# Beginning of a fused attention and two-layer kernel: three weight units and the last tokens' scores are moved

## The chip, the cores and the metric

One core of one Trainium2 chip runs the whole program. The metric is the device time of one execution in microseconds: 1802.85 us for the kernel before, the median of 3 runs (1801.82 to 1803.31).

## What is computed

Attention with keys and values summed over 8 neighbouring positions, for 8 batches of 576 tokens and 8 heads of 64; its output, 4608 rows of 512, goes through a layer with g = h cos(h), and that through a gated layer. All arrays are float32.

```
k_p = mean of k over groups of 8 positions; v_p likewise        # (B, H, 72, 64)
scores = q @ k_p.T / sqrt(64);  attn = softmax(scores);  x = attn @ v_p
x -> (4608, 512)
h = x @ w_in        (512 x 2048);   y = (h * cos(h)) @ w_out    (2048 x 512)
z = (silu(y @ w_gate) * (y @ w_val)) @ w_out2
```

Here w_in and w_out matter. They arrive as 64-bit floats and are converted on the chip.

## The kernel before, in words

The tokens are worked on in blocks of 512 columns; the first block needs the attention of batch 0 (576 tokens). The program opens with that attention, then runs 9 x 16 "slots": slot (n, f) computes one block of h (128 rows of d_ff by 512 tokens) for token block n, its cosine, and two slots later the product with w_out.

**Conversion of weights.** A generator `conv` goes through a fixed list `order` of units of 128 x 512 values: units 0 to 7 are w_in (groups 0 and 1, four row blocks each), then units of w_out ("o") and of the rest of w_in ("i") alternate. A unit is loaded as pairs of 32-bit words by SP's queue (L459) into the place that its result will have, or into one of two raw buffers for w_out. VectorE then takes six steps for a unit of w_in: mask the exponent (L466), sign (L477), mask the mantissa (L483), low word (L488), product (L494), and the low part after ScalarE has cast the high part to fp32r (L998, L1011); between the first and the second, ScalarE does a bias step (L472). Units of w_out have the first five. `fill(m)` takes m steps of the generator, and `fill_to` runs it until a given unit is done. The first masking of a unit is begun up to two units ahead. In the first 16 slots each slot calls for 8 such steps and for one unit of w_out. Units below 8 use a buffer with the tag "w" (four of them), which the rounding of turns in each slot uses too.

**Opening.** Keys, values and q of batch 0 and 1 are loaded by SP; `load_kv1` loads k and v of batch 1 into places that later hold w_in's groups 2 and 3, so those units can be loaded only when these sums are done. Then the string `program` is worked through: "s" scores and exponentials of a tile of tokens (tile 4 is the last 64), "x" its normalisation, "p" transposes of weights, "a" attention output into `ring` (L382, copied at L388), "K" and "U" sums of batch 1's k and v, "f" and "F" conversion, "X" the cut of x into a high and a low part `xhl` (ScalarE L128, VectorE L129; four row blocks), "k" the transposes of batch 1's pooled k (`prep_k`, L231 to L238), "i", "o", "q" and "b" loads. Batch 1's attention runs inside slots 1 to 16.

**Slots.** `pe_h` (L532 to L534) makes h of three fp32r products into one of two banks "hg"; `turns` scales it (ScalarE L541, a single buffer "hs"), rounds (ScalarE L543, VectorE L544); `cosine` takes sine and square (ScalarE L565, L566) and the product with h (VectorE L569). `pe_y` (L595 in the first block) multiplies with w_out. Scores, transposed weights, attention outputs and `prep_k` share two banks "att".

**Order.** Each engine works off one queue in order. What stands in it is put in order beforehand by a planner, which goes through the instructions by written order and takes, for each engine, the first one that it believes ready; so an instruction can be placed ahead of one that was written earlier. `keep_in_program_order` keeps an instruction behind the one written before it on its engine.

Of the kernel before, what the change touches and what calls it, by code (L numbers as in the profile page):

```python
# [25 lines left out]
def fused_kernel(  # L26
# [18 lines left out]
    nc = tc.nc  # L45
# [4 lines left out]
    P = 128  # L50
    POOL = 8
    SP = S // POOL
    NP = H // 2
# [4 lines left out]
    KC = DM // P  # L58
# [19 lines left out]
    ident = const.tile([P, P], F32, name="ident")  # L78
# [48 lines left out]
    def split(hi, lo, src):  # L127
        nc.scalar.copy(hi, src)  # L128
        nc.vector.tensor_sub(lo, src, hi)  # L129
# [90 lines left out]
    def sum_kv(b, kind, i):  # L220
# [2 lines left out]
        dst = vps[b][:, i] if kind == "v" else kps[b][:, i] if i < NP else kps[b][: SL * NP, i]  # L223
        pool_sum(nc.gpsimd, dst, kvraw.pop((b, kind, i)))

    def prep_k(b):

        kp = kps.pop(b)
        ps = psum.tile([P, NP * SP], F32, name=f"kps_{b}", tag="att", bufs=2)
        for g in range(2):  # L230
            nc.tensor.transpose(ps[:, g * P : (g + 1) * P], kp[:, 2 * g : 2 * g + 2].rearrange("s r d -> s (r d)"), ident)  # L231
        m = SL * NP
        nc.tensor.transpose(ps[:, 2 * P :], kp[:m, NP:].rearrange("s r d -> s (r d)"), ident[:m, :m])
        for r in range(2):
            rows = slice(r * D, (r + 1) * D)
            to = kT[rows, :, r * SP : (r + 1) * SP]
            nc.scalar.mul(to[:, :, :SM], ps[rows, : 2 * P].rearrange("d (p s) -> d p s", p=NP), -EXP_SCALE)
            nc.scalar.mul(to[:, :, SM:], ps[rows, 2 * P :].rearrange("d (s p) -> d p s", p=NP), -EXP_SCALE)  # L238
# [104 lines left out]
    def do_pt(b, t):  # L343
        pth, ptl, ptx = av_tile("pth", b), av_tile("ptl", b), av_tile("ptx", b)
        t0, n = TILES[t]
        o = t0 - GROUPS[GROUP[t]][0]
        pm = pms.pop((b, t))
        ps = psum.tile([P, NP, n], F32, name=f"pt_{b}_{t}", tag="att", bufs=2)
        for p in range(NP):
            nc.tensor.transpose(ps[:, p], pm[:n, p * P : (p + 1) * P], ident[:n, :n])  # L350
        if b < ACTB:
            nc.scalar.copy(pth[:, :, o : o + n], ps)
            px = psum.tile([SM, n], F32, name=f"px_{b}_{t}", tag="att", bufs=2)
            nc.tensor.transpose(px, pm[:n, NP * P : NP * P + SM], ident[:n, :n])
            nc.scalar.copy(ptx[:SM, o : o + n], px)
            return
        nc.scalar.copy(pth[:, :, o : o + n], ps)
        nc.vector.tensor_sub(ptl[:, :, o : o + n], ps, pth[:, :, o : o + n])
        px = psum.tile([P, n], F32, name=f"px_{b}_{t}", tag="att", bufs=2)
        nc.tensor.transpose(px, pm[:n, NP * P :], ident[:n, :n])  # L360
        nc.scalar.copy(ptx[:, o : o + n], px)
        nc.vector.tensor_sub(ptx[SM:, o : o + n], px[SM:], ptx[SM:, o : o + n])
# [143 lines left out]

    xhl = []

    def x_split(half):
        if not xhl:  # L510
            xhl.append(const.tile([P, 2, KC, TB], F32R, name="xhl", tag="xhl"))
        for c in range(KC):
            src = ring[:, c, half * TB : (half + 1) * TB]
            split(xhl[0][:, 0, c], xhl[0][:, 1, c], src)

    wa = {}
    acc = {}
# [421 lines left out]
    order = [("i", j, c) for j in range(2) for c in range(KC)][: KC + LEAD]  # L939
# [6 lines left out]
    def load_i(m):  # L946
        for _ in range(m):
            u = next(to_load_i, None)
            if u is not None:
                _, j, c = order[u]  # L950
                cv_load(keys[u], w_in[c * P : (c + 1) * P, j * TB : (j + 1) * TB], f"wa{j}{c}")
# [24 lines left out]
    def conv():  # L976

        n = len(order)
        begun = 0
        x = None  # L980
        done = -1
        for u in range(n + 1):
            if u < n:
                while begun <= u:
                    first(begun)
                    begun += 1
                    yield done
                cv_sign(keys[u])
                yield done
            if u > 0:  # L990
                x = cv_mul(keys[u - 1])
                if order[u - 1][0] == "o":
                    load_o(1)
                    done = u - 1
                else:
                    _, j, c = order[u - 1]
                    home = wa[j, c] = wts.tile([P, 2, TB], F32R, name=f"wa_{j}_{c}", tag=f"wa{j}{c}")
                    nc.scalar.copy(home[:, 0], x)  # L998
                yield done
            if u < n:  # L1000
                cv_high(keys[u])
                yield done
            while begun < min(u + 3, n) and not (order[begun][0] == order[begun - 1][0] == "o"):
                first(begun)
                begun += 1
                yield done
            if u < n:
                cv_low(keys[u])
                yield done
            if u > 0 and order[u - 1][0] == "i":  # L1010
                nc.vector.tensor_sub(home[:, 1], x, home[:, 0])  # L1011
                done = u - 1
                yield done

    wo_raw = []
    conv_ops = conv()
    conv_done = [-1]

    def fill(m):
        for _ in range(m):  # L1020
            conv_done[0] = next(conv_ops, len(order))

    def fill_to(kind, j, c):
        u = order.index((kind, j, c))
        while conv_done[0] < u:
            fill(1)
# [21 lines left out]
        pool_sum(nc.vector, kps[0][:, 2 * g : 2 * g + 2], kst[:, 2 * g : 2 * g + 2])  # L1048
    pool_sum(nc.vector, kps[0][: SL * NP, NP:], kst[: SL * NP, NP:NK])
    prep_k(0)  # L1050
    load_kv1()
    load_i(1)
    fill(8)
    do_qt(0, 0)
    kfree = kst.rearrange("s h x -> s (h x)")
# [22 lines left out]
    def sum_v1():  # L1078
# [3 lines left out]


    program = (
        "s0 s1 f4 x0 s2 p0 V0 v x1 p1 f6 s3 F3 a0 x2 p2 x3 p3 a1 w K0 K1 K2 U0 X s4 q i11 o2 "
        "x4 k b f6 "
    )
    steps = {
        "s": s_,
# [6 lines left out]
        "U": lambda t: sum_v1(),  # L1096
        "f": fill,
        "F": lambda c: fill_to("i", 0, c),
        "i": load_i,
        "o": load_o,  # L1100
        "q": lambda: load_q(1),
        "k": lambda: prep_k(1),
        "b": lambda: load_kv(*raws[0]),
        "w": lambda: wo_raw.extend(
            p1w.tile([P, 8, DM], F32, name=f"wo_{i}", tag=f"big{i}", bufs=1) for i in range(2)
        ),
        "X": lambda: x_split(0),
    }
    for step in program.split():
        steps[step[0]](*([int(step[1:])] if step[1:] else []))  # L1110
# [15 lines left out]
    for i, s in enumerate(slots):  # L1126
        n, f = s
        if s == (NB - 1, 0):
            p1a.release()
            pools2["a"] = tc.alloc_tile_pool(name="p2a", bufs=1, reuse_waits="tile")  # L1130
            tsteps = t_steps(0)
            gsteps = None
        units1, units2 = units2, []
        if n == 0:
            if f % KC == 0:
                fill_to("i", f // KC, KC - 1)
            load_i(1)
        if i + 2 in cv_slots and i % NF1 != 1:
            w2_get()
        if f == 0 and i:  # L1140
            pe_y(slots[i - 2])
        pe_h(s)
        if 2 * NF1 <= i + 1 < len(slots):
            wo_load(i + 1)
        if n == 0:
            fill(4)
        turns(s)
        if 0 < i <= NF1:
            fill_to("o", 0, i - 1)
        if i:  # L1150
            parts(slots[i - 1])
        if f == NF1 - 1 and n + 1 < NB:
            x_split((n + 1) % 2)
        if n == 0:
            fill(2)
        for u in units1:
            cv_bias(u)
        if f == 1 and n:
            pe_y(slots[i - 2])
        run_slot(mids, i)  # L1160
        if f > 1 or i == 1:
            if i >= 2:
                pe_y(slots[i - 2])
        if n == 0:
            fill(2)
        cosine(s)
        if f == 1 and n:
            y_out(n - 1)
        for u in units1:
            nc.sync.dma_start(w2_dram[w2c], cv_val(u))  # L1170
            w2c += 1
        run_slot(lates, i)
        run_slot(exps, i)
        run_slot(norms, i)
        if n == 0:
            if i == 0:
                do_pt(0, 4)
                do_qt(1, 0)
                for p in range(NP):
                    do_av(0, 2, p)  # L1180
            if i == 2:
                prep_v(1)
        else:
            if i + 2 in cv_slots and i % NF1 == 1:
                w2_get()
            if i + 1 in cv_slots:
                units2 = [f"w2_{w2c}"]
        for u in units2:
            cv_exp(u)
        if i == 2 * NF1:  # L1190
            osteps = gen_out()
        if 64 <= i < 79 or 104 <= i < 119 or 127 <= i < 142:
            run(osteps)
        if n == NB - 1:
            if f == 1:
                load_x2(0)
            if f == 2:
                gen_load(0)
            if 3 <= f < 11:
                run(tsteps)  # L1200
            if f == 8:
                gsteps = gen_steps(0)
            if f >= 8:
                run(gsteps, 2)
# [80 lines left out]
```

## Time and profile before

| | |
|---|---|
| median of 3 runs | 1802.85 us |
| the profiled execution | 1801.87 us |
| its span in the trace | 1800.1 us |
| VectorE busy | 1247.9 us (69%) |
| ScalarE busy | 1075.4 us (60%) |
| granted TensorE clock, mean | 0.993 |

The trace holds one execution. "Busy" counts instructions at work, without waits. PE is TensorE, DVE VectorE, ACT ScalarE, POOL GpSimd, SP the engine that issues transfers. Times in rows count from the start of the span.

### The profile page before, as it was taken

The page shows a single profiled execution, that of the slowest core. Times are in us where ns is not written, and L with a number is a line of the kernel's source. Part 1 is how long each engine was busy: PE and PEld are TensorE (multiplying, and loading weights), DVE is VectorE, ACT ScalarE, POOL GpSimd, SP SyncE. Part 2 cuts the span into 40 slices and gives each one's busy share as a digit, 9 for nine tenths or more (in the row PEclk, how much of TensorE's full clock was granted, in tenths as well). Part 3 has the DMA queues.
Part 4 walks back from the last instruction along what each step waited for, and adds up shares of the span by engine and source line. Part 5 has one row for each costly group of instructions (what it writes and reads, how often), then busy time and mean ns, then how long its engine had stood idle before and what let it go on. Part 6 is the DMA issues. An engine that isn't in the chain of part 4 may idle for free.

```text
span 1800.1 us, 23553 instructions
## 1 busy us (share of the span) xinstructions
PE 1743.4 (97%) x8056; PEld 1443.0 (80%) x8056; DVE 1247.9 (69%) x2147; ACT 1075.4 (60%) x1956; POOL 139.1 (8%) x218
## 2 busy tenths in 40 slices
PE   5789999999999999999999999999999999999998
PEld 3446588788878888888878888888888888999998
DVE  6598787877777777787875586863684367458346
ACT  4588578777877767778676664533443344344333
POOL 0130410403103012000000000000000000000000
PEclk9889999999999999999999999999999999999999
DMA  9634244646566454584785488576567656787773
GB/s 219 175 106 120 79 169 138 202 132 205 141 195 229 114 200 128 165 239 142 235 274 177 165 319 288 196 258 222 190 201 265 197 190 221 294 261 246 294 253 91
DMA packets 245031, 357.03 MB, mean 198 GB/s; under 512 B 146480, under 2 KB 152624, under 8 KB 244912
## 3 DMA queue, kind: packets, MB, share of 16 engines
q1 hardware_dynamic: 240224, 354.35, 61.9%
q10 hardware_dynamic: 4688, 1.18, 0.3%
q8 instruction: 64, 1.05, 0.2%
q14 instruction: 55, 0.45, 0.1%
HBM read 285.74 MB, written 69.73 MB: 197 GB/s over the span
## 4 chain that ended last, share of the span: by engine, by line
PE 75%; DVE 11%; DMA 7%; ACT 5%; issue 1%; SPq 0%; DVEq 0%; ACTq 0%
PE X L787 14%; PE oX L917 8%; PE Y L787 7%; PE h L532 5%; PE h L533 5%; PE h L534 5%; PE acc L602 5%; PE acc L603 5%; PE acc L604 5%; PE oY L917 4%; PE Z L787 4%; PE av L382 3%; PE oZ L917 2%; PE s L297 2%; PE acc L595 2%; DMA w2r<-w_dram 2%
## 5 line engine op out<-in xcount | busy, mean ns | idle before, releaser
L532 PE MATMUL h<-xhl,wa 128*128 128x512 f32 x576 | 232.2, 403 | 10.0 <-ACT hs L541 10.0
L787 PE MATMUL X<-t_P,wc 128*128 128x512 f32 (+1 forms) x1080 | 232.7, 368 | 0.8 <-ACT u L836 0.8
L533 PE MATMUL h<-xhl,wa 128*128 128x512 f32 x576 | 226.1, 392 | 0.0
L534 PE MATMUL h<-xhl,wa 128*128 128x512 f32 x576 | 225.8, 392 | 0.0
L787 PEld LDWEIGHTS X<-t_P,wc 128*128 128x128 f32 x1080 | 196.5, 188 | 27.3 <-ACT u L836 2.1
L603 PE MATMUL acc<-gl,wo_ring 128*128 128x512 f32 x448 | 176.2, 393 | 3.3 <-DVE gl L583 3.2
L604 PE MATMUL acc<-gh,wo_ring 128*128 128x512 f32 x448 | 174.9, 390 | 0.0
L602 PE MATMUL acc<-gh,wo_ring 128*128 128x512 f32 x448 | 173.4, 400 | 0.9 <-ACT gh L580 0.6
L532 PEld LDWEIGHTS h<-xhl,wa 128*128 128x128 f32 x576 | 108.8, 189 | 36.8 <-ACT hs L541 11.6
L569 DVE SCALAR_TENSOR_TENSOR w<-w,hs 128x512 f32<-128x512 f32 x144 | 101.6, 706 | 49.2 <-ACT w L566 48.1
L541 ACT ACTIVATE hs<-h 128x512 f32<-128x512 f32 x144 | 85.8, 596 | 76.5 <-DVE w L569 51.7
L534 PEld LDWEIGHTS h<-xhl,wa 128*128 128x128 f32 x576 | 108.7, 189 | 23.6 <-issue 0.5
L565 ACT ACTIVATE w<-w 128x512 f32<-128x512 f32 x144 | 91.0, 632 | 61.0 <-DVE w L544 59.9
L533 PEld LDWEIGHTS h<-xhl,wa 128*128 128x128 f32 x576 | 109.0, 189 | 23.0 <-issue 1.9
L839 DVE TENSOR_TENSOR p<-p,X 128x512 f32<-128x512 f32 (+1 forms) x60 | 37.8, 632 | 117.1 <-PE X L787 109.6
L544 DVE SCALAR_TENSOR_TENSOR w<-w,hs 128x512 f32<-128x512 f32 x144 | 103.5, 719 | 21.9 <-ACT w L543 21.9
L583 DVE TENSOR_TENSOR gl<-w,gh 128x512 fp32r<-128x512 f32 x128 | 89.5, 699 | 41.9 <-ACT gh L580 40.6
L128 ACT CAST xhl<-pst 128x1024 fp32r<-128x1024 f32 (+1 forms) x70 | 67.7, 968 | 71.1 <-PE oX L917 26.1
L543 ACT ACTIVATE w<-hs,few 128x512 f32<-128x512 f32 x144 | 104.5, 725 | 9.6 <-DMA w_dram<-ce_w 4.7
L603 PEld LDWEIGHTS acc<-gl,wo_ring 128*128 128x128 f32 x448 | 84.2, 188 | 24.0 <-DVE gl L583 7.9
L917 PE MATMUL oX<-xhl,wc 128*128 128x512 f32 (+1 forms) x480 | 102.8, 368 | 0.0
L602 PEld LDWEIGHTS acc<-gh,wo_ring 128*128 128x128 f32 x448 | 83.7, 188 | 19.9 <-ACT gh L580 3.0
(202 smaller groups left out, 3558.2 us busy)
## 6 DMA issues: line engine op xcount, KB each, us to landing
wc<-wc_dram SPq DMA_DIRECT2D x273, 512.0 KB
wo_ring<-wo_dram SPq DMA_DIRECT2D x112, 512.0 KB
wc_dram<-wc SPq DMA_DIRECT2D x42, 512.0 KB
wc_dram<-ow SPq DMA_DIRECT2D x42, 256.0 KB
y_dram<-yo SPq DMA_DIRECT2D x18, 512.0 KB
w_dram<-ce_w SPq DMA_DIRECT2D x36, 256.0 KB
st_i<-in_moe_w_in_dram SPq DMA_DIRECT2D x16, 512.0 KB
st_o<-in_moe_w_out_dram SPq DMA_DIRECT2D x16, 512.0 KB
```

Source lines behind the costliest of these rows:

```text
L532: nc.tensor.matmul(ps, whi, xhl[0][:, 0, c], start=c == 0, stop=False)
L533: nc.tensor.matmul(ps, whi, xhl[0][:, 1, c], start=False, stop=False)
L534: nc.tensor.matmul(ps, wlo, xhl[0][:, 0, c], start=False, stop=c == KC - 1)
L543: nc.scalar.activation(w, h, AF.Identity, bias=magic)
L544: nc.vector.scalar_tensor_tensor(out=w, in0=w, scalar=MAGIC, in1=h, op0=ALU.subtract, op1=ALU.subtract)
L565: nc.scalar.activation(w, w, AF.Sin, scale=PI)
L569: nc.vector.scalar_tensor_tensor(out=w, in0=w, scalar=1.0, in1=h, op0=ALU.subtract, op1=ALU.mult, reverse0=True)
L602: nc.tensor.matmul(acc[n][i], a[:, cols], xh, start=f == 0, stop=False)
L603: nc.tensor.matmul(acc[n][i], a[:, cols], xl, start=False, stop=False)
L604: nc.tensor.matmul(acc[n][i], b[:, cols], xh, start=False, stop=f == NF1 - 1)
L787: nc.tensor.matmul(ps[:, :hb], w, t[:, x, c, :hb], start=first and c == 0 and n == 0, stop=c == 1 and n == 2, skip_group_check=not first,)
L917: nc.tensor.matmul(banks[key][m][:, :hb], u, x[:, b, i, :hb], start=first_ and j == i == k == 0, stop=j == NJ - 1 and i == 1 and k == 2, s ...
```

## The change

Units 4 to 6 of w_in are loaded ahead of `load_kv1` (one of them stood behind it, two were loaded by the conversion itself), unit 7 ahead of batch 1's q; "G2" converts up to unit 6 ahead of the sums K and U and the cut X. Until X is written, no unit beyond 7 is begun (`ahead`). The last 64 tokens' scores "s4" move from behind X to ahead of the attention output "a0". `prep_k(1)` moves from behind their normalisation to behind the first slot's products. Pinned to written order: the cuts of X on both engines, the transposes in `prep_k(1)`, and those of the last 64 tokens' weights.

```diff
+    def pinned(ins, cond):
+
+        if cond:
+            tc.keep_in_program_order(ins)
...
-            nc.tensor.transpose(ps[:, g * P : (g + 1) * P], kp[...], ident)
+            pinned(nc.tensor.transpose(ps[:, g * P : (g + 1) * P], kp[...], ident), b == 1)
...
-            nc.tensor.transpose(ps[:, p], pm[:n, p * P : (p + 1) * P], ident[:n, :n])
+            pinned(nc.tensor.transpose(ps[:, p], pm[:n, p * P : (p + 1) * P], ident[:n, :n]), (b, t) == (0, 4))
...
-    def x_split(half):
+    def x_split(half, first=False):
...
-            split(xhl[0][:, 0, c], xhl[0][:, 1, c], src)
+            a = nc.scalar.copy(xhl[0][:, 0, c], src)
+            b = nc.vector.tensor_sub(xhl[0][:, 1, c], src, xhl[0][:, 0, c])
+            if first:
+                tc.keep_in_program_order(a)
+                tc.keep_in_program_order(b)
...
-            while begun < min(u + 3, n) and not (order[begun][0] == order[begun - 1][0] == "o"):
+            while begun < min(u + 3, n, ahead[0]) and not (order[begun][0] == order[begun - 1][0] == "o"):
...
+    ahead = [2 * KC]
...
+    load_i(3)
     load_kv1()
-    load_i(1)
...
-        "s0 s1 f4 x0 s2 p0 V0 v x1 p1 f6 s3 F3 a0 x2 p2 x3 p3 a1 w K0 K1 K2 U0 X s4 q i11 o2 "
-        "x4 k b f6 "
+        "s0 s1 f4 x0 s2 p0 V0 v x1 p1 f6 s3 s4 F3 a0 x2 p2 x3 p3 a1 w i1 q G2 K0 K1 K2 U0 X i11 o2 "
+        "x4 b f6 "
...
+        "G": lambda c: fill_to("i", 1, c),
...
-        "k": lambda: prep_k(1),
...
-        "X": lambda: x_split(0),
+        "X": lambda: [x_split(0, True), ahead.__setitem__(0, len(order))],
...
         pe_h(s)
+        if i == 0:
+            prep_k(1)
```

## Rows read from the trace of the kernel before

**Rows 1.** The page: busy us, share of the span and instructions of each engine.
```profile
PE 1743.4 (97%) x8056; PEld 1443.0 (80%) x8056; DVE 1247.9 (69%) x2147; ACT 1075.4 (60%) x1956; POOL 139.1 (8%) x218
```

**Rows 2.** Busy by stretch: length; PE, PEld, DVE, ACT, POOL; granted clock, DMA share, GB/s.
```profile
0.00:64.00 64.00, 41.12 (x114) 24.79 (x115) 36.26 (x84) 29.47 (x105) 4.46 (x19) 1.00 0.90 208
64.00:82.00 18.00, 15.26 (x69) 11.37 (x68) 13.10 (x28) 10.79 (x36) 3.99 (x6) 0.91 0.66 237
82.00:110.00 28.00, 17.81 (x49) 11.14 (x48) 27.19 (x54) 26.38 (x60) 3.08 (x5) 0.69 0.16 51
110.00:135.30 25.30, 20.68 (x65) 11.56 (x64) 25.30 (x39) 17.51 (x41) 16.97 (x24) 0.93 0.44 138
...
260.00:1790.00 1530.00, 1522.44 (x7267) 1298.90 (x7267) 1043.12 (x1756) 900.02 (x1536) 84.24 (x128) 1.00 0.65 209
```

**Rows 3.** Waits of PE, 64 to 135.3 us: total us, times, longest.
```profile
PE h L532 <- ACT hs L541: 8.2, 3, 7.2
PE acc L595 <- DVE wo L494: 7.2, 3, 3.2
```

**Rows 4.** Timeline of DVE, 56 to 65 us: start, us, instruction, idle before it.
```profile
56.63 0.69 DVE L129 TENSOR_TENSOR xhl<-ring,xhl 128x512 fp32r<-128x512 f32 x1 [8.88 <-ACT xhl L128]
...
59.55 0.42 DVE L466 TENSOR_SCALAR ce_i<-st_i 128x512 uint32<-128x512 uint32 x1
...
64.34 0.68 DVE L477 SCALAR_TENSOR_TENSOR ce_i<-st_i,ce_i 128x512 uint32<-128x512 uint32 x1
64.94 0.68 DVE L129 TENSOR_TENSOR xhl<-ring,xhl 128x512 fp32r<-128x512 f32 x1
```

**Rows 5.** Timeline of DVE, 71 to 102 us.
```profile
71.68 0.68 DVE L332 TENSOR_TENSOR pm<-e,sm 64x512 f32<-64x512 f32 x1
...
77.69 0.68 DVE L247 TENSOR_TENSOR vl<-vp,few 64x512 f32<-64x512 f32 x1 [1.36 <-PE av L382]
...
96.92 0.41 DVE L466 TENSOR_SCALAR wo<-st_o 128x512 uint32<-128x512 uint32 x1
...
101.64 0.41 DVE L483 TENSOR_SCALAR st_o<-st_o 128x512 uint32<-128x512 uint32 x1
101.98 0.67 DVE L494 SCALAR_TENSOR_TENSOR wo<-st_o,wo 128x512 f32<-128x512 f32 x1
```

**Rows 6.** Timeline of SP's queue, 33 to 65 us.
```profile
33.69 2.36 SPq L459 DMA_DIRECT2D st_i<-in_moe_w_in_dram  x3
...
63.86 0.93 SPq L459 DMA_DIRECT2D st_o<-in_moe_w_out_dram  x2
```

**Rows 7.** Timeline of PE, 40 to 65 us.
```profile
40.31 1.19 PE L382 MATMUL av<-pth,vmh 128*128 128x256 f32 x2 [1.90 <-DVE kst L339]
...
62.38 2.18 PE L297 MATMUL s<-kT,qT 128*64 128x144 f32 x8
64.49 0.77 PE L532 MATMUL h<-xhl,wa 128*128 128x512 f32 x1
```

**Rows 8.** Timeline of ACT, 38 to 111 us.
```profile
38.89 0.32 ACT L307 ACTIVATE kst<-s,mx 128x72 f32<-128x72 f32 x1
...
41.28 0.65 ACT L998 CAST wa<-ce_i 128x512 fp32r<-128x512 f32 x1
...
71.06 0.60 ACT L541 ACTIVATE hs<-h 128x512 f32<-128x512 f32 x1
...
78.89 0.72 ACT L543 ACTIVATE w<-hs,few 128x512 f32<-128x512 f32 x1
...
82.74 1.28 ACT L565 ACT_TABLE_LOAD   x1
...
89.25 0.59 ACT L541 ACTIVATE hs<-h 128x512 f32<-128x512 f32 x1
...
110.21 1.28 ACT L565 ACT_TABLE_LOAD   x1
```

**Rows 9.** Timeline of POOL, at 77 us.
```profile
77.06 1.64 POOL L207 TENSOR_TENSOR kraw<-kraw 128x256 f32<-128x256 f32 x2 [71.65 <-DMA kraw<-in_k_dram]
```

More of the change, by code (lines that the diff above doesn't have):

```diff
@@ L230, in prep_k @@
         for g in range(2):
-            nc.tensor.transpose(ps[:, g * P : (g + 1) * P], kp[:, 2 * g : 2 * g + 2].rearrange("s r d -> s (r d)"), ident)
+            pinned(nc.tensor.transpose(ps[:, g * P : (g + 1) * P], kp[:, 2 * g : 2 * g + 2].rearrange("s r d -> s (r d)"), ident), b == 1)
         m = SL * NP
-        nc.tensor.transpose(ps[:, 2 * P :], kp[:m, NP:].rearrange("s r d -> s (r d)"), ident[:m, :m])
+        pinned(nc.tensor.transpose(ps[:, 2 * P :], kp[:m, NP:].rearrange("s r d -> s (r d)"), ident[:m, :m]), b == 1)
         for r in range(2):
```

## The prediction

> **What bounds the kernel now.** I read the busy shares first: TensorE works 1743.4 of 1800.1 us [rows 1], so about 57 us are TensorE idle, and only an edit that gives some of those back can move the time. The table by stretch says where they are [rows 2]: 22.9 us before 64 us, 2.7 us between 64 and 82, 10.2 us between 82 and 110, 4.6 us between 110 and 135.3; from 260 to 1790 us only 7.6 of 1530 us. So a microsecond won before 135 us is carried to the end by a TensorE that is full from there, and one lost is carried as well.
>
> What holds TensorE between 64 and 135? VectorE: 27.19 of 28.0 us busy between 82 and 110 and all 25.3 us after that [rows 2]. The waits of TensorE in that stretch end on the scaling of h (8.2 us in all, longest 7.2) and on the last step of a converted row block of w_out (7.2 us) [rows 3]. Both are late because VectorE is late. ScalarE is the next in line (26.38 of 28.0 us between 82 and 110 [rows 2]). A second cost shows in the granted clock, 0.69 between 82 and 110: after the 7.2 us wait the products run at the lower of its two levels (1.2 of 2.4 GHz). Ahead of 64 us it is the other way round: VectorE stood idle for 8.88 us until the first part of x was cut [rows 4], because TensorE was at the attention output until 62 us. So there is an idle VectorE directly ahead of an overloaded one.
>
> **The change part by part.**
>
> *Units 4 to 6 of w_in ahead of the cut of x.* A unit costs VectorE six steps. The start-to-start distance is what counts in a full queue: 0.60 us behind a two-input step (64.34 to 64.94 [rows 4]) and 0.34 behind a masking step (101.64 to 101.98 [rows 5]), so 4 x 0.60 + 2 x 0.34 = 3.08 us. In the kernel before, unit 4 had only its first step done (59.55) between the cuts; its second ran at 64.34, directly ahead of the fourth cut at 64.94 [rows 4], and units 5 and 6 follow. All three go in front now: 2.74 + 3.08 + 3.08 = 8.90 us leave the loaded stretch. Unit 7 goes with them as far as its own steps are written ahead (two masking, two two-input steps): 0.34 + 0.60 + 0.34 + 0.60 = 1.88 us. Its data is the last to come, so I count half, 0.94 (bounds 0 and 1.88).
>
> Do they fit in front? They need 9.24 to 11.1 us, and the gap is 8.88 us plus idle pieces between the four cuts; the first cut may slip some 2 us. It is hidden: the products can't begin before the attention output ends, and the first three cuts are needed one after the other from then on. If that cover is gone, the price is one for one.
>
> *The loads.* Three transfers of 512 KB (1.57 MB) go in front of the second batch's k and v. At 208 GB/s, the rate of the first 64 us [rows 2], that puts k and v off by 7.6 us. In the kernel before the three were issued at 33.69 us [rows 6], behind k and v, so the sum of bytes is the same up to q; q gets one more unit ahead of it, 2.5 us. The sums of k and v now stand behind the three units, some 10 us later, so a delay of 7.6 us is covered; q is read at 80 us. Everything SP issues afterwards (the other eight units, two of w_out at 63.86 us [rows 6], k of the third batch) keeps its place in bytes. Value 0; bounds 0 and 2 us.
>
> *The scores of the last 64 tokens ahead of the attention output.* Eight matmuls, 2.2 us, stood between the attention output and the first product (62.38 to 64.49 us) [rows 7] and go away there. At the new place TensorE was idle for 1.90 us ahead of 40.31 [rows 7], but the scores need the two banks in which the previous tokens' scores lie; their exponentials run from 38.89 to 41.28 us, 1.2 us for each bank [rows 8]. So: first half's scores at about 40.1 to 41.2, its reduction 0.5, its four exponentials 1.2 us, and the attention output starts at about 43.0 instead of 40.31. That is +2.7 at one end and -2.1 at the other: the first product is 0.6 us later, and the fourth cut, which hung on the previous end of the attention output, comes 1.4 us later than its 64.94. I charge VectorE's stretch 1.4 us (bounds 0, where the order puts the attention output first, and 2.7). What is behind the wait on ScalarE's queue is the copy of each attention output; they come as late as the output itself.
>
> *The last tokens' normalisation* leaves VectorE's loaded stretch with its scores: one step of 0.68 us counted [rows 5], the small ones not.
>
> *The pins* (cuts of x, transposes of k and of the last weights stay in written order). Before, the transposes of k split the first product's matmuls, and those of the last weights split the third's. Pinned, they stand behind the first product; k's sums and the normalisation are done by then. Value 0, bounds -1 and +3. One thing may get better: the first rounding of turns ran at 78.89 us, 7.8 us after its scaled input at 71.06, and the next scaling followed only at 89.25 [rows 8]; VectorE also waited 1.36 us for attention outputs at 77.69 [rows 5]. The buffers of that rounding are shared with units 4 to 7, which are gone earlier now. I count none of it in the sum.
>
> **Sum.** 8.90 + 0.94 + 0.68 - 1.4 = 9.1 us by which VectorE reaches the same place earlier; TensorE has 17.5 us idle from 64 to 135.3 [rows 2], so it can follow. The profiled execution took 1801.87 us (1.8 more than its span), which gives 1792.8; the median of the runs is 1.0 above that execution, so 1793.7.
>
> A page speaks against following so far. The Trainium skill ("ScalarE: Activation LUTs", What ACT_TABLE_LOAD costs) gives a change of table as a load of 1.28 us and a drain of 1.38 us on top. The trace has the 1.28 us load [rows 8], but not the drain: with seven loads between 82 and 112 us ScalarE had only 1.6 us idle between 82 and 110 [rows 2], where drains would need some 8. By the page ScalarE could not follow and the gain would shrink to that of rival (a); by the row it can, and I keep the sum.
>
> **Rivals.**
> (a) *ScalarE, or data of w_out, takes VectorE's place.* From 64 to 110 us ScalarE is busy 37.2 of 46 us [rows 2]; squeezed by 9 us, with the last tokens' eight exponentials gone (2.4 us) and three units' casts and bias steps (a cast is 0.65 us; some 3 in all), it would be at 32 of 37, with table loads between its steps [rows 8]. And the first unit of w_out, first read at 96.92 us [rows 5], lands late: what was queued behind it was waited for until 77.06 [rows 9]. If VectorE comes to it at 67, it stands up to 8 us. Gain 10.1 with all of unit 7, less 6 to 8 us: 1798 to 1801. For it: both rows; against: two units of w_in that have landed stand ready to be put in between.
> (b) *More than the sum*: the late chain rounding-scaling (18 us from 71.06 to 89.25) falls to its own length, VectorE's idle of 4.9 us between 64 and 82 [rows 2] goes too, and TensorE's clock stays up: 9.1 + 4.9 = 14 us, 1789 and as far as 1784.
> (c) *Slower: an unlanded unit of w_out stands in VectorE's queue ahead of the last cuts of x.* The queue is in order, and the order is made by a planner. If the first masking of w_out is put between the cuts, the cuts wait for its landing, which I put at 75.5, shortly before the transfer behind it [rows 9], and the fourth ends at 77.7 instead of 65.5: +12.2 us. With the relief of 10.5 cut to 8 by ScalarE that is 4 us slower: 1807. It decides from a landing after 73 us. Against: the written order has that unit behind the cuts, and the planner placed it late before.
> (d) *It does not do what it says*: the planner already ran the units when it could and does so again; 1802.5.
>
> **How the numbers follow.** Forecast 0.45 (its own range 1789 to 1798), (b) 0.17, (a) 0.22, (c) 0.13, (d) 0.03. No change means within 0.2%, 3.6 us, about what a measurement of this kernel can tell. Faster: forecast, (b) and a third of (a), 0.70; same: the rest of (a) and (d), 0.17; slower 0.13. The range takes in the forecast, (a), (d) and most of (b): 1784 to 1804.
>
> **What would show it.** Right: VectorE's idle ahead of the first cut shrinks from 8.88 to under 2 us and is filled by steps of w_in; the first product starts between 64 and 66; the wait of 7.2 us on the scaling shrinks; VectorE's fully busy stretch ends near 126 instead of 135; TensorE's idle falls in 64 to 135 alone. Wrong: an idle VectorE in 60 to 80 us that ends on w_out's landing (a, c), ScalarE with no idle from 70 to 100 us (a), a first product after 70 us (c).

## The result: 0.75% slower, and the profile after

The kernel after takes 1816.26 us (median of 4 runs, 1814.64 to 1818.61), against 1802.38 us for the kernel before on the same chip: ratio 1.0075, 95% interval 1.0063 to 1.0087, or 13.9 us slower. The forecast was 1793.7 us and a gain of 9.1. The trace of after is that of its longest execution (1818.61 us). Lines from 231 on stand 5 to 9 further down now: L471 masks the exponent, L499 is the product of a conversion, L520 VectorE's part of the cut, L541 to L543 the products of h, L604 those with w_out.

The page's busy row of after, then busy time by stretch with the columns of [rows 2]:

```profile
PE 1748.7 (96%) x8056; PEld 1443.9 (79%) x8056; DVE 1246.1 (69%) x2147; ACT 1069.8 (59%) x1952; POOL 149.1 (8%) x218
```

```profile
0.00:64.00 64.00, 37.43 (x108) 22.82 (x108) 45.98 (x105) 31.82 (x120) 4.46 (x19) 1.00 0.80 186
64.00:82.00 18.00, 18.00 (x62) 12.07 (x62) 5.56 (x11) 9.40 (x22) 0.00 (x0) 1.00 0.90 301
82.00:110.00 28.00, 16.47 (x71) 12.23 (x70) 16.68 (x34) 16.95 (x39) 5.90 (x9) 0.89 0.03 11
110.00:135.30 25.30, 18.33 (x43) 9.17 (x44) 22.82 (x44) 15.40 (x37) 7.88 (x11) 0.79 0.34 105
...
260.00:1790.00 1530.00, 1520.68 (x7239) 1294.88 (x7238) 1042.12 (x1759) 904.66 (x1547) 81.97 (x128) 1.00 0.65 209
```

Against [rows 2]: VectorE did 9.7 us more ahead of 64 us (45.98 for 36.26), as forecast. But from 64 to 110 us, where it was to be the bound, it now works only 22.2 of 46 us (40.3 before). It did not come to the same place earlier; it stood still. The transfers were not what it waited for: from 82 to 110 us the DMA engines are busy 3% of the time.

VectorE's timeline of after, 71 to 111 us, shows what it did instead:

```profile
71.55 0.21 DVE L344 TENSOR_TENSOR pm<-e,sm 64x64 f32<-64x64 f32 x1
76.03 0.69 DVE L553 SCALAR_TENSOR_TENSOR w<-w,hs 128x512 f32<-128x512 f32 x1 [4.28 <-ACT w L552]
79.14 0.69 DVE L578 SCALAR_TENSOR_TENSOR w<-w,hs 128x512 f32<-128x512 f32 x1 [2.41 <-ACT w L575]
82.49 0.68 DVE L252 TENSOR_TENSOR vl<-vp,few 64x512 f32<-64x512 f32 x1 [2.66 <-PE av L387]
84.42 0.83 DVE L553 SCALAR_TENSOR_TENSOR w<-w,hs 128x512 f32<-128x512 f32 x1 [1.25 <-ACT w L552]
86.62 0.72 DVE L578 SCALAR_TENSOR_TENSOR w<-w,hs 128x512 f32<-128x512 f32 x1 [1.36 <-ACT w L575]
88.81 0.69 DVE L553 SCALAR_TENSOR_TENSOR w<-w,hs 128x512 f32<-128x512 f32 x1 [1.48 <-ACT w L552]
...
95.70 0.70 DVE L290 STREAM_TRANSPOSE qT<-qi 128x512 f32<-128x512 f32 x1
...
99.31 0.42 DVE L471 TENSOR_SCALAR wo<-st_i 128x512 uint32<-128x512 uint32 x1
...
110.87 0.38 DVE L471 TENSOR_SCALAR wo<-st_o 128x512 uint32<-128x512 uint32 x1
```

Four slots' roundings and cosine products (L553, L578) follow each other with only batch 1's masked v (82.49) between them, and each waits for ScalarE. A slot's round between the two engines takes 4.2 to 4.4 us (84.42 to 88.81 is 4.39, the next, to 93.04, 4.23), of which VectorE works 1.4. Only then come the next tokens' q (95.70), the rest of w_in (99.31) and w_out (110.87, 13.95 us later than the 96.92 of [rows 5]). In the kernel before, VectorE's queue had q's transpose and unit 7's first step ahead of the first rounding, and other units between the two steps of a slot:

```profile
79.63 0.70 DVE L285 STREAM_TRANSPOSE qT<-qi 128x512 f32<-128x512 f32 x1
80.26 0.39 DVE L466 TENSOR_SCALAR ce_i<-st_i 128x512 uint32<-128x512 uint32 x1
...
82.19 0.68 DVE L544 SCALAR_TENSOR_TENSOR w<-w,hs 128x512 f32<-128x512 f32 x1
```

What TensorE waits for between 64 and 135.3 us, with the columns of [rows 3]:

```profile
PE pt L355 <- ACT e L312: 6.2, 1, 6.2
PE h L541 <- ACT hs L550: 4.2, 3, 1.8
PE acc L604 <- DVE wo L499: 3.7, 2, 3.5
```

The wait of 7.2 us on the scaling of h is gone, as forecast (longest now 1.8). In its place TensorE waits for batch 1's first exponentials, which hang on the late q. The first product with w_out starts at 116.9 us, 14.2 later than in the kernel before (102.7). By the unit of w_out that is converted eleventh the lag is 9.1 us, by the second token block's first gated products 13.7, at the end of the span 16.8 (1816.9 for 1800.1). Part of what comes behind the eleventh unit is one wait, seen in the queues of SP and TensorE:

```profile
219.45 2.51 SPq L181 DMA_DIRECT2D vraw<-in_v_dram  x3
222.05 0.54 SPq L464 DMA_DIRECT2D st_o<-in_moe_w_out_dram  x1
```

```profile
231.63 6.23 PE L604 MATMUL acc<-w,wo 128*128 128x512 f32 x8 [5.92 <-DVE wo L499]
```

The last unit of w_out is issued behind loads of v that wait for a place; TensorE stands 5.92 us for it (1.12 in the kernel before, with the load at 211.44) and does the eight products in 6.23 us at a granted clock of 0.59 (3.70 us at 1.00 before). Of the runs below, e2 (5.34) and e23 (5.63) have this wait too; with the scores back, without the pins, or with q last it was not there at this size. No run tested it by itself.

### The profile page after: what moved, and what is told of

Same layout as the page of the kernel before. It is cut to its first block, busy times and chain, and to the rows that moved or that the text cites. A ratio compares the mean times of both kernels' runs of the same rounds, so it can differ in the third digit from the quotient of the medians.

```text
span 1816.9 us, 23559 instructions
## 1 busy us (share of the span) xinstructions
PE 1748.7 (96%) x8056; PEld 1443.9 (79%) x8056; DVE 1246.1 (69%) x2147; ACT 1069.8 (59%) x1952; POOL 149.1 (8%) x218
## 4 chain that ended last, share of the span: by engine, by line
PE 74%; DVE 12%; ACT 6%; DMA 5%; issue 2%; SPq 0%; ACTq 0%; DVEq 0%
PE X L796 14%; PE oX L926 8%; PE Y L796 7%; PE h L541 5%; PE h L542 5%; PE acc L612 5%; PE acc L611 5%; PE h L543 5%; PE acc L613 4%; PE oY L926 4%; PE Z L796 4%; PE av L387 3%; PE oZ L926 2%; PE s L302 2%; DVE w L578 1%
## 5 line engine op out<-in xcount | busy, mean ns | idle before, releaser
L541 PE MATMUL h<-xhl,wa 128*128 128x512 f32 x576 | 231.8, 403 | 6.0 <-ACT hs L550 6.0
L543 PE MATMUL h<-xhl,wa 128*128 128x512 f32 x576 | 226.2, 393 | 0.0
L578 DVE SCALAR_TENSOR_TENSOR w<-w,hs 128x512 f32<-128x512 f32 x144 | 101.2, 703 | 55.1 <-ACT w L575 53.9
L541 PEld LDWEIGHTS h<-xhl,wa 128*128 128x128 f32 x576 | 108.7, 189 | 33.7 <-ACT hs L550 7.8
L543 PEld LDWEIGHTS h<-xhl,wa 128*128 128x128 f32 x576 | 108.6, 189 | 23.6 <-issue 0.7
L553 DVE SCALAR_TENSOR_TENSOR w<-w,hs 128x512 f32<-128x512 f32 x144 | 103.9, 721 | 31.2 <-ACT w L552 31.2
```

Of the source, the lines that this page charges most:

```text
L541: nc.tensor.matmul(ps, whi, xhl[0][:, 0, c], start=c == 0, stop=False)
L543: nc.tensor.matmul(ps, wlo, xhl[0][:, 0, c], start=False, stop=c == KC - 1)
L553: nc.vector.scalar_tensor_tensor(out=w, in0=w, scalar=MAGIC, in1=h, op0=ALU.subtract, op1=ALU.subtract)
L578: nc.vector.scalar_tensor_tensor(out=w, in0=w, scalar=1.0, in1=h, op0=ALU.subtract, op1=ALU.mult, reverse0=True)
```

## Experiments

All times are medians; a ratio is against the kernel before, run on the same chip. The diffs of the string `program` show only the stretch that differs.

**The three parts by themselves.** *e1*, after with the scores back behind X:

```diff
- s3 s4 F3 a0 x2 p2 x3 p3 a1 w i1 q G2 K0 K1 K2 U0 X i11 o2
+ s3 F3 a0 x2 p2 x3 p3 a1 w i1 q G2 K0 K1 K2 U0 X s4 i11 o2
```

> The changed kernel with the last 64 tokens' scores back behind the cut of x. Theory P (VectorE's queue: the planner sets the first units of w_out and the rest of w_in behind four slots' turns, because their loads stand behind q's): this order stays, so 1811 to 1818 us, and the first step of w_out still comes about 38 us after the last cut of x. Rival S (the scores delay the attention output by 6 us and everything after it): 1806 to 1810 us. Rival V (w_in's last eight loads wait for the sums of v): as P.

1810.85 us, ratio 1.0045 (1.003 to 1.006), between the two forecasts. The first masking of w_out stays at 110.77 us: the scores did not make the order. The attention output is back at 40.39 us, but the first cut of x (L520) now comes at 69.35 us, where it was at 56.63 before. VectorE's queue has the units ahead of it and waits for ScalarE's cast of one of them; TensorE then waits for the cut, inside the first product. VectorE and TensorE of e1:

```profile
61.19 0.69 DVE L1020 TENSOR_TENSOR wa<-ce_i,wa 128x512 fp32r<-128x512 f32 x1 [5.05 <-ACT wa L1007]
```

```profile
70.08 0.79 PE L542 MATMUL h<-xhl,wa 128*128 128x512 f32 x1 [4.29 <-DVE xhl L520]
```

*e4*, before with the scores moved alone (`s3 s4 F3 ... U0 X q i11 o2`):

> The kernel before with nothing but the last 64 tokens' scores moved ahead of the attention output. Rival S: 1808 to 1812 us, since undoing this in the changed kernel gave back some 8 us. Theory P: only the later start of the first product counts, and VectorE keeps its order, 1801 to 1807 us.

1804.11 us, 1.0010 (1.0000 to 1.0019). Here the attention output starts at 43.48 us, as the prediction had it (43.0).

*e10*, after without the three groups of pins (`pinned` and the pins in `x_split` do nothing):

> The changed kernel without its pins (cuts of x, transposes). Theory P: VectorE's queue keeps four turns ahead of all conversions, 1812 to 1818 us. Rival N (the pins hold the queues up): 1800 to 1808 us.

1811.28 us, 1.0050 (1.0035 to 1.0065), just under theory P's range; first masking of w_out at 111.32. The pins did not make the order either.

**Is it the loads' time?** *e2*, after with the sums ahead of the units (`w i1 q K0 K1 K2 U0 G2 X`):

> The changed kernel with batch 1's sums of k and v written ahead of the three units. Rival V: the eight loads are issued some 8 us earlier than 61.65 us, w_out's two by as much, so 1803 to 1809 us. Theory P: the order of VectorE behind the cut does not change, so 1813 to 1818 us although the loads come earlier. Rival S: 1814 to 1818.

1820.76 us, 1.0098 (1.0083 to 1.0113), above all three forecasts. The loads behind the sums were issued at 52.57 and 59.11 us, earlier than in the kernel before (53.86, and 63.86 [rows 6]), and the first product with w_out came at 119.0 all the same. So the wait of SP for the sums of v, which the trace of after shows for 9.4 us, is not what the time hangs on.

*e3*, after with w_out's two loads ahead of q (`w i1 o2 q G2 ... X i11`), and *e5*, the same in the kernel before (`X s4 o2 q i11`):

> The changed kernel with the loads of w_out's first two units put ahead of q's load. Theory P: their conversion stands directly behind the cut, the first product with w_out starts near 85 instead of 117 us, VectorE is not idle from 72 to 99 us; 1787 to 1798 us. Rival S: 1812 to 1817, since the scores stay where they are. Rival V: w_in's rest still waits for the sums of v, so the slots that need it stall: 1805 to 1815.

> The kernel before with the loads of w_out's first two units ahead of q's and of w_in's last ones, nothing else. Theory P: what the planner believes of these loads held back the kernel before too (first step of w_out at 96.9 us, though nothing else was loading after 76): 1788 to 1798 us. Rivals S and V: no difference, 1800 to 1804 us.

1805.06 us (1.0019, 1.0006 to 1.0032) and 1809.98 us (1.0041, 1.0026 to 1.0056). Theory P missed in both, by 7 and 12 us; e3's time lies at the edge of rival V's range, whose wait e2 speaks against. w_out's first two units then come early (first product with it at 82.1 and 95.6 us), but everything else still stands behind q: the third product is at 119.6 in e3, and in e5, where w_out's masking stands ahead of q in VectorE's queue, TensorE waits, between 64 and 135.3 us, 8.5 us for q's transpose and 6.6 for the cosine products.

**Load q last.** *e6*, after:

```diff
- w i1 q G2 K0 K1 K2 U0 X i11 o2 x4 b f6
+ w i1 G2 K0 K1 K2 U0 X i11 o2 q x4 b f6
```

> The changed kernel with the loads of batch 1's q put behind those of w_in's last units and of w_out's first two (they stood ahead of both); nothing else. Theory P, now more exact: the planner takes q's sixteen transfers for long, so everything loaded behind them stands behind four slots' turns in VectorE's queue. With q last, conversions stand between the turns: first step of w_out near 80 instead of 110.9 us, first product with w_out near 95 instead of 117, VectorE idle under 8 us between 72 and 99; 1792 to 1804 us. Rival S (the scores ahead of the attention output are the loss): 1812 to 1818 us.

1798.07 us, 0.9974 (0.9965 to 0.9984): faster than both kernels, as theory P had it. Busy time by stretch from 64 to 110 us, and VectorE's first steps on the rest of w_in and on w_out:

```profile
64.00:82.00 18.00, 18.00 (x62) 12.23 (x61) 12.05 (x26) 11.78 (x25) 0.00 (x0) 1.00 0.81 211
82.00:110.00 28.00, 23.15 (x79) 15.13 (x78) 26.21 (x44) 19.81 (x35) 7.97 (x9) 0.94 0.27 75
```

```profile
70.47 0.37 DVE L471 TENSOR_SCALAR wo<-st_i 128x512 uint32<-128x512 uint32 x1
...
79.49 0.42 DVE L471 TENSOR_SCALAR wo<-st_o 128x512 uint32<-128x512 uint32 x1
```

The rest of w_in starts at 70.47 us instead of 99.31 in after: VectorE works 38.3 of the 46 us. *e8* adds the scores back and w_out's load first (`s3 F3 ... w i1 o2 G2 K0 K1 K2 U0 X s4 i11 q`); *e20* adds the scores back alone (`... U0 X s4 i11 o2 q`); *e11* is the kernel before with q last (`U0 X s4 i11 o2 q x4 k b f6`).

> The changed kernel with three edits: last tokens' scores back behind the cut, w_out's first two units loaded first, q last. Theory P with the scores' delay as a second loss: 1785 to 1797 us, below the kernel before. If the early units themselves are the loss: above 1803.

> The kernel after with q loaded last and the last 64 tokens' scores back behind the cut of x. If the scores' move costs its 4 to 6 us of start also where the order is right: ratio 0.994 to 0.997. If the cut of x comes late instead, as in the run with the scores back alone (first cut at 69.3): 0.997 to 0.999, no different from the run with q last alone.

> The kernel before, with q of the next tokens loaded behind the eight units of w_in and the two of w_out, and nothing else changed. It asks what the change is worth once that load stands last (against the same edit of the kernel after, 1798.07). Theory P (the load of q in the written order is what sends everything behind it to the end of VectorE's queue; where q is last, the three units in front are worth most of their 9 us): the first masking of w_out comes before 90 us, and the time is 1799 to 1804, some 2 to 6 us above the mended after. Rival Q (the place of q alone gives the gain, and the units in front are worth nothing): 1796 to 1798.5. Rival N (with the old order q's place does nothing): 1802 to 1803.5 with the first masking of w_out still near 97 us.

e8: 1799.48 us, 0.9980 (0.9971 to 0.9990), its forecast missed. e20: 1796.79 us, 0.9969 (0.9957 to 0.9981), the best here; whether better than e6 the intervals don't say. The cut of x comes late in it, as in e1 (67.91 us, TensorE waits 4.30 us for it), and its time does not tell its two forecasts apart. e11: 1807.08 us, 1.0019 (1.0010 to 1.0029), slower than all that was expected of it, though the first masking of w_out comes at 85.48 us, as theory P had it. So the same edit that turns after into a gain makes before slower. The stretches of e20, for [rows 2]:

```profile
64.00:82.00 18.00, 13.65 (x56) 10.03 (x55) 16.43 (x39) 11.67 (x36) 0.00 (x0) 0.77 0.83 245
82.00:110.00 28.00, 23.34 (x81) 15.72 (x80) 28.00 (x48) 21.22 (x37) 14.99 (x9) 0.94 0.40 98
```

**Which edit turned the order round?** *e15*, after with one unit ahead of the sums (`G0` for `G2`):

> The kernel after, with one unit of the second group ahead of the second batch's sums instead of three. Theory P (a step of order, not of amount: the four roundings of turns stand ahead of the next tokens' q and of w_out in VectorE's queue as before): first masking of w_out between 107 and 113 us, 1810 to 1817. Rival D (the loss grows with the number of units taken out of the loaded stretch, as less is left to fill the wait for q): a third of the loss, 1804 to 1809, with the first masking of w_out near 101 to 104 us.

1814.14 us, 1.0052 (1.0036 to 1.0068), first masking at 113.47: the number of units is not it. *e12*, the kernel before with one load moved, that of unit 7:

```diff
- a1 w K0 K1 K2 U0 X s4 q i11 o2 x4 k b f6
+ a1 w i1 K0 K1 K2 U0 X s4 q i11 o2 x4 k b f6
```

> The kernel before with one edit: unit 7 of w_in is loaded ahead of the second batch's sums and so ahead of q. Theory U (that load's place against q's turns VectorE's queue round): the first masking of w_out comes past 105 us instead of 96.92, and the time is 1808 to 1818. Rival G (it takes the units' loads ahead of k and v): 1800 to 1804 with the first masking near 97 us.

1812.69 us, 1.0062 (1.0047 to 1.0076). Its VectorE, 84 to 95 us (lines of the kernel before), is that of after:

```profile
84.58 0.69 DVE L569 SCALAR_TENSOR_TENSOR w<-w,hs 128x512 f32<-128x512 f32 x1 [0.22 <-ACT w L566]
86.75 0.69 DVE L544 SCALAR_TENSOR_TENSOR w<-w,hs 128x512 f32<-128x512 f32 x1 [1.48 <-ACT w L543]
88.81 0.69 DVE L569 SCALAR_TENSOR_TENSOR w<-w,hs 128x512 f32<-128x512 f32 x1 [1.36 <-ACT w L566]
...
93.64 0.70 DVE L285 STREAM_TRANSPOSE qT<-qi 128x512 f32<-128x512 f32 x1
94.27 0.38 DVE L466 TENSOR_SCALAR wo<-st_i 128x512 uint32<-128x512 uint32 x1
```

SP's queue shows no load that was issued late enough for that: four units, then q, 1.2 us later than before (38.26 for 37.05) where its first transpose comes 14.0 us later (93.64 for 79.63), with w_out issued at 63.27 us (63.86 before, [rows 6]):

```profile
33.63 3.77 SPq L459 DMA_DIRECT2D st_i<-in_moe_w_in_dram  x4
38.26 16.95 SPq L147 DMA_DIRECT2D qi<-in_q_dram  x16
55.33 7.90 SPq L459 DMA_DIRECT2D st_i<-in_moe_w_in_dram  x8
63.27 0.93 SPq L459 DMA_DIRECT2D st_o<-in_moe_w_out_dram  x2
```

*e21* is the swap in the other direction, in after (`w q i1 G2` for `w i1 q G2`), and *e22* takes the scores back as well:

> The kernel after with one swap: the next tokens' q is loaded ahead of unit 7 of w_in instead of behind it. Theory U (unit 7's load ahead of q is what turns the order of VectorE's queue round: the planner then has the four units ready early, puts four turns' roundings first and q, the rest of w_in and w_out behind them): the first q transpose stands ahead of the first turn again, the first masking of w_out comes at 88 to 97 us, VectorE is busy over 25 of 28 us between 82 and 110, and most of the 9.1 us first forecast arrives: 1793 to 1800. Rival G (the loads of units 4 to 6 ahead of k and v turn it round): first masking of w_out past 107 us, 1810 to 1817. Rival S (the order is mended but the late start, attention output at 46.4 and first product at 68.5, eats the gain): 1800 to 1804.

> The same swap, with the last 64 tokens' scores back behind the cut of x. Attention output at 40.3, first product near 64.5. If the scores' move costs its 6 us of start also where the order is right: 1 to 4 us below the run with the swap alone, 1791 to 1797. If the cut of x comes late here as in the run with the scores back alone (first cut at 69.3, as VectorE waits for the casts of the units), there is no gain: within 1.5 us of the swap alone.

e21: 1806.45 us, 1.0015 (1.0007 to 1.0024). One swap takes back most of the loss, and VectorE is busy 25.6 of 28 us between 82 and 110; but no gain is left, the time lies in none of the three ranges, and the first masking of w_out at 98.5 was later than expected. e22: 1807.71 us, 1.0028 (1.0018 to 1.0038): without the scores' late start it is no faster; its first cut comes at 67.11 us. The waits of e21 are in VectorE's rows:

```profile
79.82 0.68 DVE L252 TENSOR_TENSOR vl<-vp,few 64x512 f32<-64x512 f32 x1 [8.38 <-PE av L387]
...
84.43 0.46 DVE L306 TENSOR_REDUCE mx<-s 128x4 f32<-128x288 f32 x1 [3.00 <-PE s L302]
```

*e23* pins that step of 8.38 us (batch 1's masked v, into the place that the last tokens' attention output reads) to its written place (`pinned(ins, b == 1)` in `prep_v`):

> The kernel after with q loaded ahead of unit 7 (1.0015 of before) and the second batch's masked v step pinned to its written place, so that it no longer stands ahead of the first q transpose in VectorE's queue. Theory W (what is left of the loss is VectorE standing behind that step for 8.4 us with its work ready): the wait of the step vanishes, the rest of w_in starts before 78 us instead of 81, and the time falls by 2 to 6 us against the run without the pin: 1799 to 1804, ratio 0.998 to 1.0005. Rival X (the next wait, of the first scores' minimum on TensorE, takes its place, as q's transpose is just as early and its scores are queued behind the third product): ratio 1.001 to 1.003, VectorE still idle for over 9 us between 64 and 82.

1810.45 us, 1.0039 (1.0025 to 1.0052). The theory of the run fell, and its rival holds in its mechanism, at a higher price than it gave: the next step takes over the whole wait, as its scores stand behind the products in TensorE's queue (84.40 us, q's transpose at 70.87). Its trace also has the wait for the last unit of w_out, 5.63 us (2.23 in e21), so the price is not the pin's alone.

```profile
85.09 0.46 DVE L307 TENSOR_REDUCE mx<-s 128x4 f32<-128x288 f32 x1 [13.21 <-PE s L303]
```

**The late start.** *e16*, after with a third buffer for the exponentials' row sums, and *e17*, the same with q last:

```diff
-                    sm = sms[b, t] = p1a.tile([P, H, 1], F32, name=f"sm_{b}_{t}", tag="sm", bufs=2)
+                    sm = sms[b, t] = p1a.tile([P, H, 1], F32, name=f"sm_{b}_{t}", tag="sm", bufs=3)
```

> The kernel after, with three buffers for the exponentials' row sums instead of two. Theory B (the last 64 tokens' exponentials waited for a row-sum buffer that the third tile's normalisation frees, and that is the 3.4 us by which the attention output came later than predicted): the attention output starts at 43.0 to 44.0 us instead of 46.4, the first product near 66.0 instead of 68.5. The turns are bound further on by the order in VectorE's queue, so little of it arrives: 1811 to 1816, the first w_out masking still past 107 us. Rival: the wait was for something else (the banks of scores, the tile of exponentials) and the attention output starts at 46 as before, 1815 to 1817.

> The kernel after, with q loaded last (1798.07 by itself) and three buffers for the row sums. Theory B: the attention output starts at 43.0 to 44.0 us, the first product near 66; with the order mended VectorE is the bound from 66 us on, so 1 to 2.5 us of it arrive: 1795.5 to 1797.5. Rival (the start does not matter, since the stretch is bound by VectorE's amount of steps): 1797.5 to 1799.

e16: 1819.13 us (1809.70 to 1819.79), 1.0072 (1.0044 to 1.0100). e17: 1800.47 us, 0.9982 (0.9972 to 0.9991). Both times lie above their forecasts. The attention output of e16 did start at 43.67 us and the first product at 65.73; then TensorE lost it again. TensorE of e16, in its fastest execution (the other three took 1818.9 us and more):

```profile
43.67 1.19 PE L387 MATMUL av<-pth,vmh 128*128 128x256 f32 x2 [0.79 <-issue]
...
65.73 1.22 PE L541 MATMUL h<-xhl,wa 128*128 128x512 f32 x2
72.60 0.79 PE L542 MATMUL h<-xhl,wa 128*128 128x512 f32 x1 [5.65 <-DVE xhl L520]
```

The cut was late, since VectorE stood 3.94 us ahead of it (at 67.90) for unit 7's bias step, which ScalarE had behind its casts of x. In e17 the cut comes at 72.04 us, and TensorE waits 5.65 us for it. *e28* (after, q last, the last tokens' attention output written directly behind X) left things as they were:

> The kernel after with q loaded last (0.9974 of before) and the last 64 tokens' weights and attention output written directly behind the cut of x, ahead of the first product instead of behind the next ones. Theory W: the masked v no longer waits for them anywhere, but it stands late in this order already, so little changes: ratio 0.995 to 0.998. Rival (TensorE does those steps in the middle of the second product and gives away what it wins): 0.997 to 1.000.

1799.19 us, 0.9976 (0.9967 to 0.9986): in both ranges.

## Why the prediction was wrong, step by step

*The loads: the step that failed.* "Value 0; bounds 0 and 2 us", "Everything SP issues afterwards ... keeps its place in bytes", and of q "one more unit ahead of it, 2.5 us". The step priced bytes. That one unit ahead of q turned the order of VectorE's queue round, and "q is read at 80 us" became 95.70: put alone into the kernel before, it costs 0.62%, where the whole change costs 0.75%, with w_out's loads issued no later. Taking it back alone in after regains 0.60%. The prediction knew that a planner makes the order, and used it in rival (c) for one instruction; for the rest it took the order of before as given. Why the planner then puts four slots ahead of q and of all that is loaded behind q is not shown; that the place of q's load in the written order decides it is.

*Units 4 to 6, 8.90 us.* The work did move ahead of the cut: the first cut waits no longer 8.88 us, and VectorE's first 64 us hold 9.7 us more. But "leave the loaded stretch" is worth something only if VectorE has other work ready there. Where it has (q last), the size comes out: all of the change but the scores takes 1.0019 (e11) to 0.9969 (e20), 0.50% or 9.0 us, and TensorE's wait on the scaling of h between 64 and 135.3 us falls from 11.6 to 5.9 us. The intervals of the two make that 0.34 to 0.66%, 6 to 12 us; the prediction's terms for these parts, 8.90 and 0.94, make 9.8. No run parts the units from the pins and k's transposes there, and e20 pays for its late cut, so that the match is this close may be luck. Where it has not (e21, e23), VectorE waits out what it saved, 8.4 + 3.0 or 13.2 us, for steps that hang on TensorE. VectorE's idle time of 4.9 us between 64 and 82 in [rows 2], which the prediction kept for rival (b) as something to win, was the sign of this.

*"Do they fit in front?" They did not.* The prediction let the first cut slip "some 2 us", hidden behind the attention output, and counted VectorE's steps alone. But the units also need ScalarE's casts, which stand in its queue behind the copies of the attention output (in e1 copies at 55.66, 57.97 and 60.27 us, each waiting for TensorE, then the cast at 60.53). In after the first cut is 8.3 us later (64.94 for 56.63), and the late attention output hides it. In every run with the units in front where that output starts before 44 us (e1, e8, e16, e17, e20, e22) TensorE waits 1.9 to 5.7 us for the cut: the case "if that cover is gone". In e16 and e17 that wait takes back the earlier start.

*The scores: the size was off, by a wait that was not looked for.* Forecast: attention output at 43.0. In after it is 46.44, the first product at 68.50 instead of 65. ScalarE and TensorE of after:

```profile
45.03 0.32 ACT L312 ACTIVATE e<-s,mx 64x72 f32<-64x72 f32 x1 [2.32 <-DVE kst L344]
```

```profile
46.44 1.19 PE L387 MATMUL av<-pth,vmh 128*128 128x256 f32 x2 [3.58 <-issue]
...
68.50 1.22 PE L541 MATMUL h<-xhl,wa 128*128 128x512 f32 x2
```

The exponentials waited for one of two row-sum buffers, which the third tile's normalisation frees; e16, with three, gives 43.67 and 65.73, near the forecast. The edit's price is 1.8 us alone (e4, an interval that begins at 0) and 0.30% between after and e1; with q last (e6 to e20) it is below what the runs can tell; without it the cut comes late.

*The pins, value 0, bounds -1 to +3.* e10 is some 5 us faster than after, but with the order unchanged; in its trace the wait for the last unit of w_out is 2.6 us instead of 5.92. Whether the pins or that wait's own chance made the difference is open.

*The rivals.* None was it. (a) put the wait on ScalarE or on w_out's data; the DMA engines were idle and ScalarE worked 16.95 of 28 us. (c) had the sign and the planner, but the wrong place: w_out stood last in VectorE's queue, not first. Of the signs named, the two that came true (VectorE's gap filled, the wait on the scaling gone) were on the steps that held; "first product at 64 to 66" and "fully busy to 126" failed, and TensorE's idle time from 64 to 135.3 us did not fall (18.5 us for 17.5).

*The table load.* The Trainium skill ("ScalarE: Activation LUTs", What ACT_TABLE_LOAD costs) puts a drain of 1.38 us on top of the load. The trace shows the load alone here too. In e6 the step behind a load of 1.28 us starts 0.02 us after its end:

```profile
77.86 1.28 ACT L574 ACT_TABLE_LOAD   x1
79.16 0.63 ACT L574 ACTIVATE w<-w 128x512 f32<-128x512 f32 x1
```

## What to carry to other kernels

Where a planner fills in-order queues, an edit of a load is an edit of the order of every engine: compare, engine by engine, what stands behind what before pricing bytes or busy time. Work taken out of a full stretch is worth its time only if what is left there can run without waiting for another engine; list what will stand first in the queue, and on whom it waits. Here the moved units were worth some 9 us against the kernel before with the same place of q (e11), since with q last the weights' conversion, which hangs on no product of TensorE, stood ready to fill the gaps; against the kernel before as it was, the best run gained 0.31%. And ask of work that is moved ahead of a deadline what it waits for on other engines, not only how long it works.

## What the runs showed of the hardware

The pace of TensorE's products rose later after a later start, and the granted clock of the profile does not tell why. In after the first ten products of h stand about 0.43 us apart, up to 72.93 us, and 0.23 us from there on; in the kernel before they stand 0.23 us apart from 65.08 us on, 0.6 us behind the first. In both, TensorE had been at the attention output for 22 us with no gap of more than 0.52 us, its pairs of matmuls 1.15 us apart. The granted clock reads 1.00 in all of these stretches. In e20 the same slow paces stand beside a granted clock of 0.50 (pairs 1.15 us apart from 42.4 to 49 us, products of h 0.43 from 68.6 to 72.2 us), and the pace of 0.23 us beside 1.00 (72.2 to 76 us); 0.50 is 1.2 GHz and 1.00 is 2.4 GHz. Whether the slow paces of before and after were the lower level too, or something else, no run shows.
